# Block-sorted attention and an eight-expert layer on one core: the third batch's queries turned by transposing transfers, its value transfers on ScalarE and GpSimd, and a weight load ahead of four heads of queries

## The chip, the cores and the metric

The kernel runs on one core of one Trainium2 chip. A core has five engines that run their own instruction streams side by side: TensorE (PE, matmuls; its weight loads are listed as PEld), VectorE (DVE), ScalarE (ACT), GpSimd (POOL) and SyncE (SP), which here only starts transfers. Transfers are carried by 16 DMA engines; a transfer is started by an instruction on SP, ACT or POOL and proceeds on its own. The metric is device time in microseconds (us) of one execution; lower is better. Times are medians of several runs, and one further execution is profiled.

## The reference

The first half is attention whose keys and values are mixed block by block with a sort matrix; the second is a layer of eight experts whose routing weights are balanced by rows and columns.

```
B, H, S, D = 4, 8, 768, 64;  8 blocks of 96 rows;  E = 8, F = 1024
P = 5 rounds of (exp(P - max), row normalise, column normalise) of sort_net   # B x H x 8 x 8
k_sorted, v_sorted = einsum('bhij,bhjcd->bhicd', P, k_blocks / v_blocks)
scores = q_block @ k_sorted_block^T / 8      # inside each block of 96
attn   = softmax(scores);  x = attn @ v_sorted_block      # -> 3072 x 512
logits = x @ w_gate;  Pm = exp(logits - max), 8 rounds of row and column normalising
out    = sum_e Pm[:, e] * (relu(x @ w1[e]) @ w2[e])       # 3072 x 512
```

## The kernel before

The four batches of the attention are numbered 0 to 3 (`bb`). For each batch `load_batch` (L72) brings v, k and q from memory, converted to bf16, into tiles `kvq` of 128 partitions by 8 heads by 384 columns (five buffers in turn); row p of a head holds six successive sequence rows, written `(kk d)`. All these loads are started by POOL, one after another, in POOL's program order.

The work on a batch goes in steps, most of them for a pair of heads `hp` (0 to 3):

- `sort_values` (L179, L181): the sort matrix, spread out into `Rt[bb]` by `build_r` (L156), is multiplied with v on PE; ACT copies the products to `vs`. Then `hop` (L172) starts eight transfers that move `vs` to `vsbt[bb % 2]` with a block of 96 rows on 96 partitions. Even ones are started by SP, odd ones by POOL.
- `keys` (k, L218 and L223): sorted keys on PE, copied by DVE into `kTs` with the head dimension on the partitions.
- `queries` (q): the queries are turned so that the head dimension lies on the partitions. For batches 0 and 1 PE turns them head by head (L196). For batches 2 and 3 POOL first copies a pair of heads into a tile `qr` that puts both heads side by side (L201, two buffers), then PE turns six blocks of 128 x 128 (L205). ACT copies the result out of PSUM into `qTs` (L208), with the order of rows restored.
- `scores` (s, L239, L247): a block's keys times its queries on PE; ACT takes the exponential into `atp`.
- `mix` (m, L257, L260, L261): the exponentials times the sorted values on PE; DVE divides by the sum of each row.
- `turn` (t, L268, L271) and `logits` (l, L283): the result is turned into `xtT` and multiplied by `w_gate`.

The string of a `plan` gives the order of these steps (k0 is the keys of pair 0, and so on). Between steps PE works on expert 0 of the second half for the batches already done: `hidden0` (L379, L381), which needs `w1`, and `output0` (L388, L396), which needs `w2`. `weave` and `run_both` set how many of its steps stand between two steps of the attention. All these PSUM tiles come from eight banks in turn.

The order on an engine is the program's order for instructions that go through `pin`; others may be moved by the framework's scheduler. `tc.issue_after(x)` puts the instructions of its block behind instruction x on the same engine. L433 uses that once: POOL copies two numbers of `vsbt[0]` into a small tile `held`, and so waits for the values of batch 0, before it starts the loads of batch 1 and of w1 and w2 of expert 0.

After the attention the remaining seven experts run as a long PE-filled loop (L601, L688) with sums and differences of operands on POOL and DVE; the change does not touch it.

Of the kernel before, what the change touches and what calls it, by code (L numbers as in the profile page):

```python
# [25 lines left out]
def kernel(  # L26
# [40 lines left out]
    def load_batch(bb, parts):  # L67
        for x, l0, n in parts:
            d, src = {"v": (vt, v), "k": (kt, k), "q": (qt, q)}[x]
            if bb not in d:  # L70
                d[bb] = kvp.tile([128, 8, 384], BF16, name="kvq", bufs=5)
            pin(nc.gpsimd.dma_start(  # L72
                out=d[bb][:, l0:l0 + n, :],
                in_=src[bb, l0:l0 + n].rearrange("h (p kk) d -> p h (kk d)", kk=6)))
# [93 lines left out]

    def hop(bb):
        for i in range(NB):  # L170
            eng = nc.gpsimd if i % 2 else nc.sync
            (pin if bb == 0 else lambda ins: ins)(eng.dma_start(  # L172
                out=mkap(vsbt[bb % 2], [[VW, 96], [1, 520]], off=i * 520),
                in_=vs[16 * i:16 * i + 16].rearrange("p kk h d -> p kk (h d)")))

# [12 lines left out]
    def queries(bb, hp, bank, qps=None):  # L188

        if qps is None:  # L190
            qps = bank([128, 6, 128], BF16)
        if bb < 2:

            for kk in range(6):
                for h in range(2):
                    pin(nc.tensor.matmul(qps[64 * h:64 * h + 64, kk, :],  # L196
                                         qt[bb][:, 2 * hp + h, kk * 64:kk * 64 + 64],
                                         Ibig, is_transpose=True, start=True, stop=True))
        else:
            qr = sp.tile([128, 6, 2, 64], BF16, name="qr", bufs=2)  # L200
            nc.gpsimd.tensor_copy(  # L201
                qr.rearrange("p kk h d -> p h kk d"),
                qt[bb][:, 2 * hp:2 * hp + 2].rearrange("p h (kk d) -> p h kk d", d=64))
            for kk in range(6):
                pin(nc.tensor.matmul(qps[:, kk, :], qr[:, kk].rearrange("p h d -> p (h d)"),  # L205
                                     Ibig, is_transpose=True, start=True, stop=True))
        qT[bb, hp] = sp.tile([128, 128, 6], BF16, name="qTs", bufs=4)
        nc.scalar.copy(qT[bb, hp], qps.rearrange("p kk c -> p c kk"))  # L208

    def keys(bb, hp, bank):  # L210

# [14 lines left out]
    at = {}  # L226
# [4 lines left out]
    def scores(bb, hp, bank):  # L231

        for b in range(2):
            sps = [bank([128, 4, 96], F32) for h in range(2)]
            for j in range(4):
                i = 4 * b + j
                for h in range(2):
                    r = slice(64 * h, 64 * h + 64)
                    pin(nc.tensor.matmul(  # L239
                        sps[h][0:96, j, :],  # L240
                        kT[bb, hp][r, i].rearrange("p c kk -> p (c kk)"),
                        qT[bb, hp][r, 16 * i:16 * i + 16].rearrange("p c kk -> p (c kk)"),
                        start=True, stop=True))
            for h in range(2):
                if b == 0:
                    new_at(bb, hp, h)
                nc.scalar.activation(out=at[bb, hp, h][0:96, 4 * b:4 * b + 4],  # L247
                                     in_=sps[h][0:96], func=AF.Exp, scale=scale)

    def mix(bb, hp, h, bank):  # L250
        if h == 0:
# [208 lines left out]
    with ExitStack() as c2:  # L460
# [22 lines left out]
        def run_both(a, counts):  # L483
            for n in counts:
# [9 lines left out]
        run_both(at1, (1, 1, 1, 1, 0, 1, 0, 1, 1, 0, 1))  # L494
        load_batch(2, [(x, 0, 8) for x in "vkq"])
        build_r(2, nc.gpsimd, 4)
        run_both(at1, (1, 1, 1, 1))
        run_both(sort_values(2, bank1), (1, 0, 1, 0, 1))
        run_both(at1, (1, 0, 0, 0))
        usual = "q0,q1,k0 k1,s0,q2 k2,s1,q3 m0 k3,s2 m1,t0 s3 m2,t1 m3 t2 t3,l0 l3"  # L500
        for bb, ns in ((2, (5, 3, 2, 4)), (3, (5, 4, 0, 5))):
            at1 = attention(bb, bank1, usual)
            weave(at1, ex, 5, ns[0])
            if bb + 1 < B:
                load_batch(bb + 1, [(x, 0, 8) for x in "vkq"])
                build_r(bb + 1, nc.gpsimd, 4)
# [12 lines left out]
            weave(at1, ex, 4, ns[3])  # L519
# [311 lines left out]
```

## Time and profile before

| what | value |
|---|---|
| median of 3 runs | 679.78 us (679.38 to 680.32) |
| profiled execution, own time | 679.37 us |
| its span | 677.4 us |
| PE busy | 651.2 us, 96% |
| DVE, ACT, POOL busy | 541.6 (80%), 298.2 (44%), 473.5 (70%) us |
| granted TensorE clock | full in every slice |
| attention, first to last turn into xtT | ends near 112 us |

The span is the stretch from the first to the last recorded instruction; the own time of the execution adds what lies around it. In the order of time a line gives the start and the length in us, the engine, the source line, what is written from what, how many instructions were merged, and in square brackets how long the engine sat idle before them and what ended that. PSUM tiles are named `bank`, `bk` or `oacc`. A transfer's landing is counted from the start of the instruction that starts it.

### The profile page before, as it was taken

How to read it: one execution, taken by the hardware profiler on the slowest of the kernel's cores; microseconds unless marked ns; L12 is line 12 of the kernel's file. 1: busy time of each engine (PE TensorE's matmuls, PEld its weight loads, DVE VectorE, ACT ScalarE, POOL GpSimd, SP SyncE). 2: the span in 40 equal slices, each digit the busy share in tenths (PEclk: the TensorE clock that was granted, in tenths of full speed). 3: DMA queues.
4: the chain of work that ended last, by engine and by line, in shares of the span. 5: the costliest groups of instructions: out<-in, count | busy, mean ns of one | idle time of the engine just before them, and what ended most of it. 6: DMA issues, size and time to landing. Idle time of an engine off the chain costs nothing.

```text
span 677.4 us, 13154 instructions
## 1 busy us (share of the span) xinstructions
PE 651.2 (96%) x5043; PEld 434.7 (64%) x5122; DVE 541.6 (80%) x1131; ACT 298.2 (44%) x541; POOL 473.5 (70%) x499
## 2 busy tenths in 40 slices
PE   4899999999999999999999999999999999999996
PEld 2656766554666666666666666666666666666675
DVE  6617768663788889888888889888898888888896
ACT  4575763469533343434333343333433343333430
POOL 4542435007987988898997898689886999646745
PEclk9999999999999999999999999999999999999999
DMA  9898973101240340030303040034003120001223
GB/s 159 143 215 132 160 133 47 19 1 24 40 62 1 63 63 1 1 63 10 55 1 57 7 64 1 2 63 63 1 1 64 19 45 1 0 1 63 94 78 141
DMA packets 32415, 36.57 MB, mean 54 GB/s; under 512 B 2016, under 2 KB 25312, under 8 KB 32352
## 3 DMA queue, kind: packets, MB, share of 16 engines
q0 software_dynamic: 26912, 27.82, 25.9%
q1 hardware_dynamic: 5440, 7.90, 3.6%
q8 instruction: 40, 0.66, 0.4%
q14 instruction: 23, 0.19, 0.1%
HBM read 52.45 MB, written 6.29 MB: 87 GB/s over the span
## 4 chain that ended last, share of the span: by engine, by line
PE 72%; DVE 1%; issue 1%; POOL 1%; ACT 0%; DVEq 0%
PE oacc L688 37%; PE bk L601 34%; PE bk L688 1%; DVE osbl L653 1%; POOL hs L671 1%; DVE hT L637 0%; DVE hT L640 0%; ACT p L621 0%; DVEq L653 0%
## 5 line engine op out<-in xcount | busy, mean ns | idle before, releaser
L653 DVE SCALAR_TENSOR_TENSOR osbl<-oacc,glog,osbl 128x256 f32<-128x256 f32 (+1 forms) x490 | 255.6, 522 | 61.3 <-PE oacc L688 61.2
L671 POOL TENSOR_TENSOR hs<-hT 128x512 bf16<-128x512 bf16 (+2 forms) x105 | 99.5, 961 | 68.4 <-DVE hT L640 68.2
L601 PE MATMUL bk<-xtT,w1e 128*128 128x512 bf16 x475 | 143.5, 379 | 0.9
L688 PEld LDWEIGHTS <-hT 128*128 128x128 bf16 x1008 | 98.6, 98 | 64.5 <-issue 1.3
L688 PEld LDWEIGHTS <-hs 128*128 128x128 bf16 x1008 | 98.5, 98 | 64.6 <-POOL hs L671 1.5
L688 PE MATMUL oacc<-w2e,hT 128*128 128x256 bf16 x796 | 119.6, 273 | 1.0 <-ACT hT L643 0.5
L643 ACT ACTIVATE hT<-bk 128x512 bf16<-128x512 f32 x84 | 50.3, 599 | 158.7 <-PE bk L601 140.9
L671 POOL TENSOR_TENSOR hs<-hT,hs 128x512 bf16<-128x512 bf16 (+2 forms) x105 | 100.0, 959 | 4.9
L671 POOL TENSOR_TENSOR hs<-hs,hT 128x512 bf16<-128x512 bf16 (+2 forms) x105 | 99.9, 959 | 4.2 <-ACT hT L643 0.4
L601 PE MATMUL bk<-xc,wc 128*128 128x512 bf16 x319 | 96.2, 379 | 0.6 <-ACT p L621 0.2
L688 PE MATMUL oacc<-w2e,hs 128*128 128x256 bf16 x612 | 92.0, 273 | 1.6 <-POOL hs L671 0.9
L629 ACT COPY u<-bk 128x512 f32<-128x512 f32 x84 | 49.3, 587 | 95.2 <-PE bk L601 83.6
L601 PEld LDWEIGHTS <-w1e 128*128 128x128 bf16 x672 | 65.7, 98 | 10.5
L637 DVE CUSTOM_DVE_ANT_0 hT<-bk,p 128x512 bf16<-128x512 f32 x84 | 58.1, 692 | 11.8 <-ACT p L634 6.4
L647 DVE SCALAR_TENSOR_TENSOR h<-bk,hT 128x512 bf16<-128x512 f32 x84 | 57.2, 681 | 5.7 <-ACT hT L643 5.7
L634 ACT COPY p<-bk 128x512 f32<-128x512 f32 x84 | 49.4, 588 | 23.5 <-PE bk L601 23.5
L621 ACT COPY p<-bk 128x512 f32<-128x512 f32 x84 | 49.4, 588 | 20.1 <-PE bk L601 20.1
L625 DVE CUSTOM_DVE_ANT_0 hT<-bk,p 128x512 bf16<-128x512 f32 x84 | 57.2, 681 | 1.1 <-ACT hT L381 0.6
L640 DVE CUSTOM_DVE_ANT_0 hT<-bk,u 128x512 bf16<-128x512 f32 x84 | 57.2, 680 | 1.0 <-PE bk L601 1.0
L688 PE MATMUL oacc<-w2s,hs 128*128 128x256 bf16 x364 | 54.8, 273 | 0.3
L601 PEld LDWEIGHTS <-wc 128*128 128x128 bf16 x504 | 49.3, 98 | 8.0 <-issue 0.4
L601 PE MATMUL bk<-xtT,wc 128*128 128x512 bf16 x159 | 48.0, 379 | 0.0
(136 smaller groups left out, 827.9 us busy)
## 6 DMA issues: line engine op xcount, KB each, us to landing
w2e<-in_moe_w_dram POOLq DMA_DIRECT2D x8, 1024.0 KB, 8.8
w1e<-in_moe_w_dram POOLq DMA_DIRECT2D x7, 1024.0 KB, 8.3
out_dram<-osbl SPq DMA_DIRECT2D x23, 256.0 KB, 2.0
kvq<-in_v_dram POOLq DMA_DIRECT2D x3, 768.0 KB, 9.0
kvq<-in_k_dram POOLq DMA_DIRECT2D x3, 768.0 KB, 11.6
vsb<-vs SPq DMA_DIRECT2D x16, 97.5 KB, 4.5
vsb<-vs POOLq DMA_DIRECT2D x16, 97.5 KB, 4.0
kvq<-in_q_dram POOLq DMA_DIRECT2D x4, 384.0 KB, 9.6
```

The costliest lines, as they stand in the source:

```text
L601: hold(nc.tensor.matmul(ps, wa[:, kk, :], xa[:, kk, :], start=(first and kk == 0), stop=(kk == 1), skip_group_check=True))
L621: nc.scalar.copy(p1, u)
L625: nc.vector._custom_dve(TENSOR_ADD_SAT, out=c11, in0=w, in1=p1, s0=TOP, s1=0.0)
L629: nc.scalar.copy(u2, u)
L634: nc.scalar.copy(p5, v)
L637: nc.vector._custom_dve(TENSOR_ADD_SAT, out=c22, in0=u, in1=p5, s0=TOP, s1=0.0)
L640: nc.vector._custom_dve(TENSOR_ADD_SAT, out=c12, in0=v, in1=u2, s0=TOP, s1=0.0)
L643: nc.scalar.activation(out=c21, in_=u, func=AF.Relu)
L647: nc.vector.scalar_tensor_tensor(out=h3[e, p][:, i, :], in0=u, scalar=0.0, in1=c22, op0=ALU.max, op1=ALU.subtract)
L653: nc.vector.scalar_tensor_tensor(out=o, in0=ps, scalar=glog[:, t, e:e + 1], in1=o, op0=ALU.mult, op1=ALU.add)
L671: nc.gpsimd.tensor_tensor(out=c, in0=a, in1=b, op=o)
L688: nc.tensor.matmul(ps, h[:, fb, :], w[:, fb, :], start=(first and fb == 0), stop=(fb == 3), skip_group_check=True)
```

## The change

Three things change, all in the attention.

1. Batch 2's queries. A new function `queries_across` lets POOL make all four `qr` copies one after another (four buffers instead of two) and lets SP start four transposing transfers from `qr` into `qTs`. `qTs` of batch 2 has its columns in the order (kk c), so the scores take a strided slice of it, their columns come out in that order too, and the exponential reads PSUM at a stride to put them right. The q steps leave the plan of batch 2. POOL's copy of two numbers of the last turned tile into `held` now stands before the loads of batch 3, which are issued behind it. `build_r(2)` stands ahead of batch 2's loads.
2. Batch 2's value transfers: the four that SP started are started by ACT. All transfers of `hop` are now pinned, as are the `qr` copies; on POOL batch 3's four `qr` copies thereby come after batch 3's value transfers instead of two on either side.
3. The loads of batch 1: w2 of expert 0 is loaded ahead of heads 4 to 7 of the queries, and the plan of batch 1 has s1 ahead of q2, and s2 ahead of q3.

In the built order of DVE, one of the differences `xc` (L146) now stands behind four of batch 2's key copies (L223) instead of ahead of them.

```diff
     def hop(bb):
         for i in range(NB):
-            eng = nc.gpsimd if i % 2 else nc.sync
-            (pin if bb == 0 else lambda ins: ins)(eng.dma_start(
+            eng = nc.gpsimd if i % 2 else nc.scalar if bb == 2 else nc.sync
+            pin(eng.dma_start(
...
-            qr = sp.tile([128, 6, 2, 64], BF16, name="qr", bufs=2)
-            nc.gpsimd.tensor_copy(
+            qr = sp.tile([128, 6, 2, 64], BF16, name="qr", bufs=4)
+            pin(nc.gpsimd.tensor_copy(
...
+    def queries_across(bb):
+        for hp in range(4):
+            qr = sp.tile([128, 6, 2, 64], BF16, name="qr", bufs=4)
+            pin(nc.gpsimd.tensor_copy(
+                qr.rearrange("p kk h d -> p h kk d"),
+                qt[bb][:, 2 * hp:2 * hp + 2].rearrange("p h (kk d) -> p h kk d", d=64)))
+            qT[bb, hp] = sp.tile([128, 6, 128], BF16, name="qTs", bufs=4)
+            pin(nc.sync.dma_start_transpose(
+                out=qT[bb, hp], in_=qr.rearrange("p kk h d -> p (kk h d)")))
...
-                        qT[bb, hp][r, 16 * i:16 * i + 16].rearrange("p c kk -> p (c kk)"),
+                        (qT[bb, hp][r, :, 16 * i:16 * i + 16] if bb == 2 else
+                         qT[bb, hp][r, 16 * i:16 * i + 16].rearrange("p c kk -> p (c kk)")),
...
+                to, of = at[bb, hp, h][0:96, 4 * b:4 * b + 4], sps[h][0:96]
+                if bb == 2:
+                    to = to.rearrange("p j (c kk) -> p j c kk", kk=6)
+                    of = of.rearrange("p j (kk c) -> p j c kk", kk=6)
+                nc.scalar.activation(out=to, in_=of, func=AF.Exp, scale=scale)
...
-            load_batch(1, [("v", 0, 8), ("k", 0, 8), ("q", 0, 4), ("q", 4, 4)])
+            load_batch(1, [("v", 0, 8), ("k", 0, 8), ("q", 0, 4)])
             load_w2(0)
+            load_batch(1, [("q", 4, 4)])
...
-        at1 = attention(1, bank1, "k0 k1 k2 q0 q1 s0 q2 s1 k3 q3 s2 "
+        at1 = attention(1, bank1, "k0 k1 k2 q0 q1 s0 s1 q2 k3 s2 q3 "
...
+        build_r(2, nc.gpsimd, 4)
         load_batch(2, [(x, 0, 8) for x in "vkq"])
-        build_r(2, nc.gpsimd, 4)
         run_both(at1, (1, 1, 1, 1))
+        queries_across(2)
         run_both(sort_values(2, bank1), (1, 0, 1, 0, 1))
...
-            at1 = attention(bb, bank1, usual)
+            at1 = attention(bb, bank1, usual if bb == 3 else
+                            "k0 k1,s0 k2,s1 m0 k3,s2 m1,t0 s3 m2,t1 m3 t2 t3,l0 l3")
...
-                load_batch(bb + 1, [(x, 0, 8) for x in "vkq"])
+                turned = pin(nc.gpsimd.tensor_copy(held, qT[2, 3][0:96, 5, 0:2]))
+                with tc.issue_after(turned.ins):
+                    load_batch(bb + 1, [(x, 0, 8) for x in "vkq"])
```

More of the change, by code (lines that the diff above doesn't have):

```diff
@@ L199, in queries @@
         else:
-            qr = sp.tile([128, 6, 2, 64], BF16, name="qr", bufs=2)
-            nc.gpsimd.tensor_copy(
+            qr = sp.tile([128, 6, 2, 64], BF16, name="qr", bufs=4)
+            pin(nc.gpsimd.tensor_copy(
                 qr.rearrange("p kk h d -> p h kk d"),
-                qt[bb][:, 2 * hp:2 * hp + 2].rearrange("p h (kk d) -> p h kk d", d=64))
+                qt[bb][:, 2 * hp:2 * hp + 2].rearrange("p h (kk d) -> p h kk d", d=64)))
             for kk in range(6):
@@ L208, in queries @@
         nc.scalar.copy(qT[bb, hp], qps.rearrange("p kk c -> p c kk"))
+    def queries_across(bb):
[3 more added lines that the diff above has]
+                qr.rearrange("p kk h d -> p h kk d"),
+                qt[bb][:, 2 * hp:2 * hp + 2].rearrange("p h (kk d) -> p h kk d", d=64)))
+            qT[bb, hp] = sp.tile([128, 6, 128], BF16, name="qTs", bufs=4)
+            pin(nc.sync.dma_start_transpose(
+                out=qT[bb, hp], in_=qr.rearrange("p kk h d -> p (kk h d)")))
     def keys(bb, hp, bank):
@@ L246, in scores @@
                     new_at(bb, hp, h)
-                nc.scalar.activation(out=at[bb, hp, h][0:96, 4 * b:4 * b + 4],
-                                     in_=sps[h][0:96], func=AF.Exp, scale=scale)
+                to, of = at[bb, hp, h][0:96, 4 * b:4 * b + 4], sps[h][0:96]
[3 more added lines that the diff above has]
+                nc.scalar.activation(out=to, in_=of, func=AF.Exp, scale=scale)
     def mix(bb, hp, h, bank):
@@ L491 @@
         run_both(sort_values(1, bank1), (1, 1, 1, 1, 0))
-        at1 = attention(1, bank1, "k0 k1 k2 q0 q1 s0 q2 s1 k3 q3 s2 "
+        at1 = attention(1, bank1, "k0 k1 k2 q0 q1 s0 s1 q2 k3 s2 q3 "
                                   "m0 s3 m1,t0 m2,t1 m3 t2 t3,l0 l3")
-        run_both(at1, (1, 1, 1, 1, 0, 1, 0, 1, 1, 0, 1))
+        run_both(at1, (1, 1, 1, 1, 0, 1, 1, 0, 1, 1, 0))
+        build_r(2, nc.gpsimd, 4)
         load_batch(2, [(x, 0, 8) for x in "vkq"])
-        build_r(2, nc.gpsimd, 4)
         run_both(at1, (1, 1, 1, 1))
+        queries_across(2)
         run_both(sort_values(2, bank1), (1, 0, 1, 0, 1))
```

## The prediction

> **What bounds the kernel now.** First the page: the chain that ended last is TensorE (PE) for 72% of the span, and PE is near full in every slice but the first. So a change is worth what it takes out of, or puts into, PE's own order.
>
> ```profile
> PE   4899999999999999999999999999999999999996
> PE 72%; DVE 1%; issue 1%; POOL 1%; ACT 0%; DVEq 0%
> ```
>
> Next PE in order of time from 40 to 95 us, the stretch that the change touches (start, length, engine, line, what, idle before):
>
> ```profile
> 46.88 0.56 PE L239 MATMUL bank<-qTs,kTs 64*96 64x96 bf16 x16
> 48.60 1.02 PE L388 MATMUL bank<-w2e,hTs 128*128 128x512 bf16 x3 [1.17 <-DMA w2e<-in_moe_w_dram]
> ...
> 69.45 0.83 PE L205 MATMUL bank<-Ibig,qr 128*128 128x128 bf16 x12
> 70.21 0.53 PE L218 MATMUL bank<-R,kvq 128*64 128x128 bf16 x12
> ...
> 71.88 0.56 PE L239 MATMUL bank<-qTs,kTs 64*96 64x96 bf16 x16
> 72.37 0.51 PE L205 MATMUL bank<-Ibig,qr 128*128 128x128 bf16 x6
> 72.72 0.81 PE L379 MATMUL bank<-xtT,w1e 128*128 128x384 bf16 x4
> ...
> 74.72 0.49 PE L205 MATMUL bank<-Ibig,qr 128*128 128x128 bf16 x6 [0.24 <-ACT qTs L208]
> 75.05 0.81 PE L379 MATMUL bank<-xtT,w1e 128*128 128x384 bf16 x4
> 75.70 0.87 PE L257 MATMUL bank<-vsb,atp 96*96 96x65 bf16 x16
> ...
> 92.15 0.83 PE L205 MATMUL bank<-Ibig,qr 128*128 128x128 bf16 x12
> ```
>
> PE waits 1.17 us for w2. From start to next start, the L205 turns of batch 2 (the third) take 0.76 + 0.35 + 0.33 us, with 0.24 us of waiting. Batch 3's turns come at 92.15 with no wait. Then GpSimd (POOL) in the same order: its first copy waits for the q load, and the next batch's load is issued behind the last copies.
>
> ```profile
> 62.73 2.22 POOL L201 COPY qr<-kvq 128x768 bf16<-128x768 bf16 x2 [13.07 <-DMA kvq<-in_q_dram]
> 65.89 2.15 POOL L172 DMA_DIRECT2D vsb<-vs  x4 [0.94 <-ACT vs L181]
> ...
> 72.16 0.93 POOL L72 DMA_DIRECT2D kvq<-in_v_dram  x1
> ...
> 88.86 1.59 POOL L201 COPY qr<-kvq 128x768 bf16<-128x768 bf16 x2 [11.90 <-PE bank L268]
> ```
>
> Last the transfers: the SP queue over the span, the landing of batch 3's q (issued 73.96), and that of batch 2's value transfers.
>
> ```profile
> q1 hardware_dynamic: 5440, 7.90, 3.6%
> kvq<-in_q_dram POOLq DMA_DIRECT2D x1, 768.0 KB, 14.4
> vsb<-vs POOLq DMA_DIRECT2D x4, 97.5 KB, 4.0
> DMA to landing us min/median/max: 2.8/4.0/5.5
> ```
>
> From the first issue of batch 3's load to the landing of its q are 73.96 + 14.4 - 72.16 = 16.2 us; PE asks for the product two copies (1.6 us) and a little later. There the slack is small.
>
> **The change, part by part.**
>
> *w2 ahead of four heads of queries.* w2 landed at 48.54 (28.84 + 19.7). The half load of q that now stands behind it is 384 KB; at the 200 GB/s that the transfers reach there it takes 1.9 us, so w2 lands near 46.6, before PE asks at 47.43 (48.60 - 1.17). Saved: 1.17. That half now lands near 48.5; its turn (L196) stands behind s0, half an output, s1 and half an output, at about 49.65. The new order puts s1's four exponentials (0.41 each) ahead of q2's copy on ScalarE (ACT), so s2 waits some 0.35 us; but before, the same stretch up to 56.38 held 0.42 us of small gaps beyond its work (7.78 against 5 x 0.86 + 3 x 0.46 + 2 x 0.49 + 0.70 = 7.36). I take 1.2 saved, bounds 0.8 to 1.4.
>
> *Batch 2's turns off PE.* 0.76 + 0.35 + 0.33 + 0.24 = 1.7 us leave PE before the first mix (75.70). Next to be late is kT for s0: PE would come 0.3 us before DVE's copies of it, which in the new order start when the logits copy ends (70.15), as one 0.69 us xc difference now stands behind four of them: 70.15 + 1.1 = 71.25, against 71.02. So 1.6 saved, bounds 1.3 to 1.7. The four ACT copies (0.80 each) also go.
>
> *What hides the rest.* Sixteen exponentials read PSUM at a stride: ACT's strided L208 copy and its straight L271 copy both took 0.80 for 768 columns, so nothing; ACT, busy 7.6 of 8 us from 72 to 80, loses two copies there. Were the stride to cost 10%, it would be 0.6 us on ACT. Four value transfers move to ACT: 0.57 to 0.70 each on SP, so 2.3 to 2.8 us behind the last values copy, where ACT sat idle 4.45; behind them waits the next hidden copy, which PE makes only near 69.7. On POOL, build_r (2.1 us) goes ahead of batch 2's load: k and q then land by the idle-queue times of batch 3 (11.4 and 14.4 after issue) at 59.3 and 63.2 instead of 58.9 and 62.7; k is first used after 68. Its cover is the backlog of w2 up to 48.5.
>
> *The new chain.* Four copies in a row at 1.1 us (62.73 row) end at 67.1 to 67.6. POOL's half of the value transfers follows: issued 67.1 to 69.3 instead of 65.9 to 68.0, landing (2.8 to 5.5) 72.1 to 74.8, middle 73.3. Mix 0 wants them at 75.70 - 1.2 - 1.6 = 72.9, the last some 0.3 later: a wait of 0 to 1.6, about 0.1. Then POOL's `held` copy waits for the fourth transposing transfer, and behind it stands all of batch 3's load. Call its landing T4. Batch 3's first turn should come at 92.15 - 2.8 = 89.35, the second six at 89.7, so q must land by 88.1 and T4 be at most 88.1 - 16.2 - 0.25 = 71.65. Every later us costs PE one us; waits at mix 0 or at the scores are inside that, not added, since they move the deadline. hop(3) on POOL (2.15) ahead of the copies fits between 84.9, when the values are out of ACT, and q's landing.
>
> *T4* has no row of its own: four transfers of 196 KB. Lower end: the value transfers' rate. 0.79 MB of turns and 0.80 MB of value transfers at the best 250 GB/s of that stretch is 6.3 us from 64.4, so 70.7; the last, issued at 67.1 plus the shortest landing 2.8, gives 69.9: T4 near 70.7. Upper end: by the piece. The SP queue's row gives 0.036 x 677.4 x 16 / 5440 = 72 ns a packet; if each 128-column block of a row is a packet, 768 a transfer over 16 engines are 3.45 us, four 13.8, T4 = 64.0 + 13.8 + about 0.7 = 78.5. SP issuing six blocks a transfer at its 0.57 gives the same 3.4. I take 72.5, nearer the low end, because the nearest row is the value transfer (same queue, SBUF to SBUF, the same bytes in all), with a tail for shorter pieces. It costs 72.5 - 71.65 = 0.85.
>
> **Sum.** Against the profiled execution: 679.37 (span 677.4 and 1.97 around it) - 1.2 - 1.6 + 0.85 = 677.4. The median of the runs, 679.78, lies 0.41 above that execution: 677.8. After 115 us the order is the old one and PE bound, so the gain should arrive at the end whole.
>
> **Rivals.**
> 1. *Turns as fast as value transfers* (T4 up to 71.65): no new wait, 679.8 - 2.8 = 677.0, and 676.6 with both savings at their upper bounds. For it: 250 GB/s in the value transfers. Against: shorter pieces. [...]
> 2. *The wait eats the gain* (T4 73.1 to 75.8): 679.8 - 2.8 + 2.8 = 679.8 at 74.45.
> 3. *The other side: the transfers are slow by the piece.* T4 78.5, load issued 78.75, q in at 95.0, the copies at 96.6; PE's second six would be at 96.6 instead of 92.5: +4.1, 683.9. It decides from T4 = 75.8 on (2.8 + 1.36 behind 71.65). For it: the packet price; against: transfers of many packets overlap in the queue.
> 4. *Blocks one at a time.* If each of the 24 blocks of 128 x 128 were a transfer waited for alone, at the trace's shortest landing on SP (1.7, sort_net), 41 us: T4 105, +31, 710. Nothing in the trace serializes a queue so. [...]
>
> **Chances.** Main case (T4 71.65 to 73.1) 0.30; rival 1 0.17; rival 2 0.16; rival 3 and its neighbours from T4 75.8 to 79 0.29; rival 4 0.04; beyond rival 3, or a wait I have not seen, 0.04. A change of 0.2% (1.36 us) is about what a measurement tells from none: faster 0.47, within 0.16, slower 0.37. Time 677.8, its own range 677.0 to 678.4. Both signs are live, so the range runs from 676.6 to the piece price, 684.0, leaving out rival 4 and what is beyond.
>
> **What would show it.** The w2 wait before L403's first matmul gone; no L205 between 68 and 80; s0 about 70; the first mix near 73. The four landings on SP against 70.4, 71.8, 74.7 and 77.6, when the scores want them. POOL's load issue: at 72 or 73 I am right, at 79 rival 3 is; the price stands on PE as idle time before batch 3's first turns, released by a copy or the q load. Wrong altogether if ACT is held by its four issues past 70, or if the exponentials of batch 2 are longer than 0.41.

## The result, and the profile after

The change made the kernel slower: 682.52 us against 679.85 us for the kernel before, measured on the same chip, 2.7 us by the medians. The recorded ratio, here and below, is not the quotient of the medians; it is 1.0032 with a 95% interval of 1.0021 to 1.0044. Its executions also scatter more, from 679.61 to 684.68 (679.34 to 682.79 before). The profiled execution took 683.75 us (span 681.5), 4.4 us more than the one profiled before (679.37) and 1.2 us more than the median, so the trace shows an execution somewhat longer than most. Since the diff adds lines, the same instructions carry other line numbers in the changed kernel: L379 is L394, L388 is L403, L218 is L229, L239 is L250, L257 is L272.

First the chain of the page, then PE in order of time, in the changed kernel:

```profile
PE 71%; DVE 1%; issue 1%; POOL 1%; ACT 0%; DVEq 0%
```

```profile
48.27 1.02 PE L403 MATMUL bank<-w2e,hTs 128*128 128x512 bf16 x3 [0.64 <-DMA w2e<-in_moe_w_dram]
...
69.55 0.53 PE L229 MATMUL bank<-R,kvq 128*64 128x128 bf16 x12
...
71.21 0.56 PE L250 MATMUL bank<-qTs,kTs 64*96 64x96 bf16 x16
...
74.06 0.33 PE L272 MATMUL bank<-vsb,atp 96*96 96x65 bf16 x4
76.12 0.28 PE L272 MATMUL bank<-vsb,atp 96*96 96x65 bf16 x2 [1.73 <-DMA vsb<-vs]
77.93 0.59 PE L272 MATMUL bank<-vsb,atp 96*96 96x65 bf16 x10 [1.53 <-DMA vsb<-vs]
78.36 0.82 PE L394 MATMUL bank<-xtT,w1e 128*128 128x384 bf16 x4
...
80.69 1.46 PE L394 MATMUL bank<-xtT,w1e 128*128 128x384 bf16 x4
...
87.47 0.48 PE L179 MATMUL bank<-kvq,R 128*128 128x384 bf16 x2 [0.46 <-DMA kvq<-in_v_dram]
...
96.05 0.51 PE L205 MATMUL bank<-Ibig,qr 128*128 128x128 bf16 x6
96.81 0.51 PE L205 MATMUL bank<-Ibig,qr 128*128 128x128 bf16 x6 [0.26 <-POOL qr L201]
```

The chain is still PE's, a point less of it: PE still sets the end, and what was lost must stand on PE as waits or as slower work. Up to the first mix all went as planned: no L205 stands between 68 and 80, and the mix begins at 74.06 against 75.70, 1.64 us earlier. Then PE waits twice inside that one mix, 1.73 + 1.53 = 3.26 us, and for the values, not for a query. What follows is slow too: four hidden matmuls (L394) take 1.46 us at 80.69 where they take 0.82 elsewhere. The windows say why; after the busy us of PE, PEld, DVE, ACT and POOL, the last three figures are the granted clock of PE, the DMA engines' share (over 1 where packets overlap) and GB/s:

```profile
74.00:76.00 2.00, 0.39 (x6) 0.24 (x4) 0.18 (x1) 1.53 (x5) 0.00 (x0) 1.00 0.56 56
76.00:78.00 2.00, 0.35 (x5) 0.28 (x5) 0.00 (x0) 0.00 (x0) 0.00 (x0) 1.00 1.01 148
78.00:80.00 2.00, 2.00 (x28) 1.38 (x29) 1.80 (x8) 0.49 (x1) 1.19 (x3) 0.78 0.00 0
80.00:82.00 2.00, 2.00 (x21) 1.29 (x22) 0.86 (x2) 1.52 (x4) 2.00 (x3) 0.50 0.66 46
82.00:84.00 2.00, 2.00 (x29) 1.55 (x27) 1.42 (x7) 0.59 (x2) 1.77 (x2) 0.87 1.27 196
```

PE is nearly idle from 74 to 78, and from about 79 to 82.5 it gets half its clock, which is 0.22 x 2 + 0.50 x 2 + 0.13 x 2 = 1.7 us of full clock. By the starts of the same matmuls it cost 1.25 us: from the hidden matmuls behind the mix (78.36, before 76.41) to the first turn into xtT (L283 at 82.92, before L268 at 79.72) PE's delay grew from 1.95 to 3.20 us. In the kernel before the clock is full throughout (1.00 in every window from 60 to 86).

The transfers, from the answers on the two lines that start them (the transposing ones at L218, then batch 2's values at L172), and POOL in order of time:

```profile
L218 SPq DMA_TRANSPOSE qTs<-qr x4: 1217/2067/2898, 65.0 to 70.8; - x4
DMA to landing us min/median/max: 2.9/6.7/10.2
```

```profile
L172 ACTq DMA_DIRECT2D vsb<-vs x4: 677/980/1387, 65.6 to 68.5; - x4
L172 POOL DMA_DIRECT2D vsb<-vs x4: 532/540/555, 67.2 to 68.8; - x4
DMA to landing us min/median/max: 3.5/6.5/9.4
```

```profile
63.61 3.66 POOL L214 COPY qr<-kvq 128x768 bf16<-128x768 bf16 x4 [13.78 <-DMA kvq<-in_q_dram]
67.22 2.11 POOL L172 DMA_DIRECT2D vsb<-vs  x4
78.47 0.18 POOL L523 COPY held<-qTs 96x2 bf16<-96x2 bf16 x1 [9.14 <-DMA qTs<-qr]
79.00 0.91 POOL L72 DMA_DIRECT2D kvq<-in_v_dram  x1 [0.35 <-issue]
```

The values took up to 9.4 us from issue to landing (5.5 before), and the third transposing transfer 10.2. In the trace the four transposing transfers are complete at 67.90, 72.31, 78.05 and 78.41, the values on ScalarE at 69.10, 71.19, 76.08 and 77.89, those on GpSimd at 72.45, 73.04, 76.03 and 77.68. The two kinds are in flight together from 66 to 78. Issuing a transposing transfer costs SP 1.33 and 1.22 us for the first two and 2.80 and 2.90 for the last two. Batch 3's load goes out at 79.00 instead of 72.16, and PE waits 0.46 + 0.26 us more for that; by the starts of the same matmuls the two places cost 0.62 + 0.54 = 1.16 us. The page's row of SP's queue went from 5440 packets to:

```profile
q1 hardware_dynamic: 8192, 8.29, 4.2%
```

The four value transfers that left SP are 448 packets (they stand on ScalarE's queue now), so the transposing transfers brought 8192 + 448 - 5440 = 3200, 800 each.

### The profile page after: what moved, and what is told of

It is laid out like the page before. It is cut to its first block, busy times and chain, and to the rows that moved or that the text cites. A ratio compares the mean times of both kernels' runs of the same rounds, so it can differ in the third digit from the quotient of the medians.

```text
span 681.5 us, 13099 instructions
## 1 busy us (share of the span) xinstructions
PE 651.9 (96%) x5019; PEld 434.2 (64%) x5098; DVE 541.9 (80%) x1131; ACT 295.8 (43%) x537; POOL 472.3 (69%) x500
## 3 DMA queue, kind: packets, MB, share of 16 engines
q1 hardware_dynamic: 8192, 8.29, 4.2%
## 4 chain that ended last, share of the span: by engine, by line
PE 71%; DVE 1%; issue 1%; POOL 1%; ACT 0%; DVEq 0%
PE oacc L708 37%; PE bk L621 34%; PE bk L708 1%; DVE osbl L673 1%; POOL hs L691 1%; DVE hT L657 0%; DVE hT L660 0%; ACT p L641 0%; DVEq L673 0%
```

## The theory, and what would tell it from others

My theory after this reading: the loss is the *meeting* of the transposing transfers with the values' transfers, which slow each other down, then PE's idle time, which halves its clock. Rivals: the transposing transfers are slow by themselves; the values are slow because ScalarE issues them or because two hardware queues (SP's and ScalarE's) run at once; the w2 order is worth nothing; the clock falls for some reason other than PE's idle time.

### The w2 order alone

The kernel before, with part 3 of the change:

```diff
-            load_batch(1, [("v", 0, 8), ("k", 0, 8), ("q", 0, 4), ("q", 4, 4)])
+            load_batch(1, [("v", 0, 8), ("k", 0, 8), ("q", 0, 4)])
             load_w2(0)
+            load_batch(1, [("q", 4, 4)])
...
-        at1 = attention(1, bank1, "k0 k1 k2 q0 q1 s0 q2 s1 k3 q3 s2 "
+        at1 = attention(1, bank1, "k0 k1 k2 q0 q1 s0 s1 q2 k3 s2 q3 "
```

> The kernel before with one part of the change alone: w2 loaded ahead of four heads of batch 1's queries, and batch 1's plan with s1 ahead of q2 and s2 ahead of q3. The prediction's step was 1.2 us saved. In the profile of the changed kernel w2's last piece came at 48.23, so that PE still waited 0.64 us for it, 0.28 us for the queries behind it and some for s2, and nothing was left of the saving by s3. Theory 'the order of loads is worth what was predicted, and one late engine took it in that one execution': 0.6 to 1.2 us below the kernel before. Rival 'the saving only moves to the next waits (the query load and s2)': within 0.3 us of before.

Measured: 678.46 us against 679.9 for the kernel before on that chip, ratio 0.9983 (0.9967 to 1.0). PE in order of time, where w2 is first used:

```profile
47.66 1.04 PE L388 MATMUL bank<-w2e,hTs 128*128 128x512 bf16 x4
48.62 0.56 PE L239 MATMUL bank<-qTs,kTs 64*96 64x96 bf16 x16
```

The wait for w2 is gone. The saving is 1.4 us by the medians and 1.3 by the means, a little over what was expected, though the interval just reaches 1. In the profiled execution of the changed kernel it did not show, since there 15 of the 16 parts of w2 had landed by 45.91 and the last only at 48.23. Of the thirteen profiled executions with this order, one for each kernel of this document but the first, three had such a wait (0.64, 0.43 and 1.13 us). So the saving is there in most executions and not in all.

### The value transfers on ScalarE, queries still turned on PE

The last kernel, with ScalarE as the issuer of batch 2's even value transfers:

```diff
-            eng = nc.gpsimd if i % 2 else nc.sync
+            eng = nc.gpsimd if i % 2 else nc.scalar if bb == 2 else nc.sync
```

> The same, and the even value transfers of batch 2 started by ACT instead of SP; the queries of batch 2 stay on PE, so no transposing transfer is in flight. If starting transfers on ACT is itself a burden (it took 4.1 us for four in the changed kernel), ACT is late for batch 2's first query copies (70.0 in the kernel before) and the time is 1 us or more above e1. If those 4.1 us came from meeting the transposing transfers, the four issues take 2.3 to 2.8 us here, the values land in 2.8 to 5.5 us, and the time is within 0.3 us of e1.

Measured: 678.92 us, ratio 0.9976 (0.9964 to 0.9988). The line that starts the values:

```profile
L172 ACTq DMA_DIRECT2D vsb<-vs x4: 606/682/772, 64.2 to 66.4; - x4
DMA to landing us min/median/max: 3.0/4.4/6.0
```

No wait at the first mix, and ScalarE issues in 0.6 to 0.8 us, not in up to 1.39 as beside the transposing transfers. The time is 0.46 us above the run before by the medians and 0.2 below it by the means, so no loss shows. ScalarE as issuer, without transposing transfers, is therefore not the cause; what the changed kernel lost lies in part 1 of the change, with the transposing transfers.

### The two kinds kept apart: values held behind the transposing transfers

The changed kernel; GpSimd and ScalarE each read two numbers of the last turned tile before they issue a value transfer:

```diff
     def hop(bb):
+        if bb == 2:
+            pin(nc.gpsimd.tensor_copy(held, qT[2, 3][0:96, 5, 0:2]))
+            pin(nc.scalar.copy(held_act, qT[2, 3][0:96, 5, 0:2]))
```

> The changed kernel with batch 2's value transfers held on both engines until the fourth transposing transfer has landed, so that the two kinds never meet. Theory 'meeting': the transposing transfers are quick by themselves (the first, alone, landed 2.9 us after its issue) and slow only beside the value transfers. Then the four issues take about 1.3 us each, the fourth lands at 71.5 to 73 instead of 78.4, the values land 3 to 5.5 us after their issue, near 77, and PE still waits some 3 us at mix 0: time 681.5 to 684. Rival 'the turns are slow by themselves from the third on' (their issues took 2.8 and 2.9 us): the fourth lands at 76 or later here too, the values after 81, time 685 or more.

Measured: 683.95 us, ratio 1.0059 (1.0038 to 1.008). The transposing transfers, now alone:

```profile
L221 SPq DMA_TRANSPOSE qTs<-qr x4: 1210/1211/1332, 65.1 to 69.4; - x4
DMA to landing us min/median/max: 2.8/2.8/4.4
```

This is the line that decides between "slow by themselves" and "meeting": alone a transposing transfer is issued in 1.21 us (the first in 1.33) and lands 2.8 us after the start of its issue in the median, 4.4 at most (6.7 and 10.2 beside the values). The fourth landed at 73.79 in place of 78.41, a little past the 71.5 to 73 expected and well short of the rival's 76. The values, issued only from 73.8 on, landed in 4.1 us (median), but the last at 80.53 and not at 73.30 as before the change, and ScalarE's next hidden copy stood behind their issues. PE waits for that copy in one piece, and the kernel is slower still:

```profile
77.02 1.44 PE L398 MATMUL bank<-xtT,w1e 128*128 128x384 bf16 x4 [5.10 <-ACT hTs L400]
```

The clock falls to 0.5 again, from 76.0, before that wait is over, to 82.9.

### All eight value transfers on GpSimd

The changed kernel with another issuer:

```diff
-            eng = nc.gpsimd if i % 2 else nc.scalar if bb == 2 else nc.sync
+            eng = nc.gpsimd if i % 2 or bb == 2 else nc.sync
```

> The changed kernel with all eight value transfers of batch 2 started by POOL, none by ACT, still beside the transposing transfers. Theory 'meeting' (any transfer beside the transposing ones): the fourth transposing transfer lands after 75, a value transfer still takes 7 us or more, PE waits 2 us or more at mix 0, time 681 to 684. Rival 'it is the two hardware queues, SP's and ACT's, that hold each other up': with ACT's queue empty the fourth lands by 73, the values (last issue near 71.5) by 76, PE waits at most 1.5 us, time 679 to 680.5.

Measured: 681.42 us, ratio 1.0019 (1.0007 to 1.0032). PE in the first mix:

```profile
73.48 0.23 PE L272 MATMUL bank<-vsb,atp 96*96 96x65 bf16 x1 [0.17 <-DMA vsb<-vs]
74.09 0.19 PE L272 MATMUL bank<-vsb,atp 96*96 96x65 bf16 x1 [0.38 <-DMA vsb<-vs]
75.06 0.19 PE L272 MATMUL bank<-vsb,atp 96*96 96x65 bf16 x1 [0.79 <-DMA vsb<-vs]
76.11 0.55 PE L272 MATMUL bank<-vsb,atp 96*96 96x65 bf16 x9 [0.86 <-DMA vsb<-vs]
```

With nothing on ScalarE's queue, PE still waits 0.17 + 0.38 + 0.79 + 0.86 = 2.2 us for the values, the last two transposing transfers still cost SP 2.0 and 3.0 us to issue, and the fourth landed at 76.26. So the pair of hardware queues is not needed for the loss; the kinds meet whoever issues them. It is milder here, though: no value transfer took over 6.3 us, where at least 7 was expected (9.4 in the changed kernel), and the time is 1.1 us below the changed kernel's. What that difference is due to stays open.

### The meeting moved to where there is slack: queries loaded first

Batch 2's v had landed by 55.8 and is read at 61.6 in the changed kernel, its k by 59.7 and at 69.6. So the queries can be loaded, copied and turned ahead of both, and the transposing transfers meet these loads instead of the values. The changed kernel, in another order:

```diff
-        load_batch(2, [(x, 0, 8) for x in "vkq"])
-        run_both(at1, (1, 1, 1, 1))
-        queries_across(2)
+        load_batch(2, [(x, 0, 8) for x in "qvk"])
+        queries_across(2)
+        run_both(at1, (1, 1, 1, 1))
```

> The changed kernel with batch 2's queries loaded first (q, v, k in place of v, k, q) and the four copies and transposing transfers moved up right behind these loads, so that they meet the loads of v and k, 8 us of slack before anything of them is needed, and no longer the transfers of the values. In the changed kernel the v of batch 2 had landed by 55.8 and is first read at 61.6, k by 59.7 and first read at 69.6. Theory (the loss of the change is the meeting of the transposing transfers with the values' transfers, and the halved clock behind PE's wait for them): the transposing transfers land between 59 and 66, the values' by 72.5 as where the queries were turned on PE; PE waits under 0.3 us at the first mix, the granted clock stays 1.0 at 76 to 84, the load of batch 3 goes out by 72.5; all of the 1.6 us of PE work removed is then gained on top of the 1.4 us of the w2 order: 678.5 - 1.6 = 676.9 us (676.3 to 677.8). Rival (transposing transfers slow down whatever else flows, the loads too, by the 4 to 6 us that the values lost): v or k lands 4 us late, PE waits for v at 61.6 or k at 69.6 by 1 to 4 us, and the time is 679 to 683.

Measured: 677.14 us against 679.75, ratio 0.9964 (0.9953 to 0.9976). This is faster than both kernels. The two lines that start the transfers, and PE and POOL in order of time:

```profile
L218 SPq DMA_TRANSPOSE qTs<-qr x4: 1328/1884/3299, 57.0 to 64.0; - x4
DMA to landing us min/median/max: 3.8/7.4/8.9
```

```profile
L172 ACTq DMA_DIRECT2D vsb<-vs x4: 606/644/970, 65.9 to 68.3; - x4
DMA to landing us min/median/max: 3.0/4.2/5.1
```

```profile
74.33 0.87 PE L272 MATMUL bank<-vsb,atp 96*96 96x65 bf16 x16
```

```profile
68.39 0.91 POOL L72 DMA_DIRECT2D kvq<-in_v_dram  x1
```

Both sides of the theory can be read here. The transposing transfers are as slow as in the changed kernel (7.4 us median, up to 3.3 us to issue), because they now meet the loads, and the last of the three loads lands 2 us later (65.60 against 63.55). But nobody is waiting for either: the transposing transfers are complete at 65.88, 66.54, 67.20 and 67.81, over three microseconds before the first scores. The values are back at 4.2 us, the first mix runs without a gap, the clock is full (1.00 in every window from 60 to 88), and batch 3's load goes out at 68.39. So the rival was right in that loads and transposing transfers slow each other too, and wrong about the price: a load came 2 us later, not 4 to 6, and nobody waited. (The 74.33 holds 1.13 us of waiting for w2, one of the three executions named above.) This kernel also has the pinned orders and the moved `build_r` of the change, so these are not what cost the changed kernel its time.

### The same order of loads with the queries on PE

The kernel with the w2 order and ScalarE as issuer, whose queries are turned on PE:

```diff
-        load_batch(2, [(x, 0, 8) for x in "vkq"])
+        load_batch(2, [(x, 0, 8) for x in "qvk"])
```

> All queries turned on PE as before the change, with the w2 order, the values' transfers on ScalarE and GpSimd, and batch 2's queries loaded first; against the kernel with the same order of loads whose queries are turned by transposing transfers (677.1 us). Theory (that kernel's gain is the 1.6 us of PE work that the transfers took over; the order of the loads alone gives nothing, since no query, key or value of batch 2 was waited for): within 0.4 us of the kernel with the queries on PE and the loads in the old order, 678.5 to 679.0 us. Rival (the order of the loads itself is the gain): 677.0 to 677.5 us.

Measured: 679.08 us against 679.61, ratio 0.9985 (0.9972 to 0.9998), the same as in the old order (678.92). The order of the loads gives nothing by itself. The difference to the kernel above, 679.08 - 677.14 = 1.9 us (1.4 to the one below, on the same chip), is what the transposing transfers are worth when they are in nobody's way; the prediction's term for it was 1.6.

### Issuer back on SP, queries first

The kernel with the queries loaded first:

```diff
-            eng = nc.gpsimd if i % 2 else nc.scalar if bb == 2 else nc.sync
+            eng = nc.gpsimd if i % 2 else nc.sync
```

> The kernel with the queries loaded first and turned by transfers (677.1 us), its even value transfers of batch 2 back on SP, where they are issued behind the four transposing transfers (the last of these issued by 65.9 in that kernel, when the first values were ready). Theory (with the transposing transfers out of the values' way, ScalarE as issuer is worth nothing): 677.1 us, 676.7 to 677.6, no wait over 0.3 us at the first mix. Rival (SP is held by its transposing transfers past 66 and the values come late): a wait of 0.5 to 2 us at the first mix, 677.7 to 680 us.

Measured: 677.71 us, ratio 0.9964 (0.9953 to 0.9976). By its median that is 0.1 us above the theory's range and 0.57 above the kernel with ScalarE as issuer (0.3 by the means), which the scatter of six executions each (ranges of 1.7 and 1.6 us) doesn't tell from nothing. The trace has none of the rival's wait: the first mix runs without a gap, and SP is through with its last transposing transfer at 64.7, before the first value transfer is issued at 64.8. So no gain from ScalarE as issuer shows here.

### Half the turns, behind the values' issues

The changed kernel with pairs 0 and 1 turned on PE again, and the other two meant to be held by a copy that reads one number of each landed piece:

```diff
+        gate = pin(nc.gpsimd.tensor_copy(
+            landed, mkap(vsbt[0], [[VW, 96], [520, 8]], off=519)))
-        for hp in range(4):
+        for hp in (2, 3):
...
+            with tc.issue_after(gate.ins):
+                pin(nc.sync.dma_start_transpose(
```

> The changed kernel with head pairs 0 and 1 of batch 2 turned on PE as before the change and pairs 2 and 3 by transposing transfers that are held (by a GpSimd copy that reads one element of each of the eight landed pieces) until the values have landed. Theory (meeting): the values land by 72.5 as with all queries on PE, the two transposing transfers are issued at about 71 to 72.5 at 1.2 to 1.3 us each and land by 76, before their scores (about 76 and 80); no wait over 0.3 at the first mix, clock 1.0; PE has 0.8 us less to do than with all four turned on it, and batch 3's load goes out at about 76 in place of 72, which costs 0 to 1.5 us: 678.5 - 0.8 + 0.4 = 678.1 us (677.4 to 679.4). Rival (the transfers are slow by themselves): the second lands past 78, PE waits for it at the third or fourth scores, the load goes out past 78, and the time is 680 to 682.

Measured: 679.11 us, ratio 0.9989 (0.9974 to 1.0004), near the upper end of what the theory gave. But the hold did not hold. `issue_after` orders instructions of the same engine, and the copy is GpSimd's while the transfers are SP's. In the trace SP issues both before the copy has run:

```profile
L225 SPq DMA_TRANSPOSE qTs<-qr x2: 1210/1629/2048, 69.1 to 71.3; - x2
71.69 0.19 POOL L220 COPY landed<-vsb 96x8 bf16<-96x8 bf16 x1 [1.88 <-DMA vsb<-vs]
```

The first went out at 69.08, when six of the eight value transfers were still in flight, and took SP 2.05 us to issue; the second followed at 71.30, and the last value landed at 71.55. They landed 3.3 and 2.7 us after issue, the values in 4.1 (median, 5.0 at most), and there was no wait at the mix. So the kinds were not kept apart here, and a meeting of some 2.5 us with one transposing transfer did the values no harm that shows. PE lost its gain elsewhere (L257 is the scores in this kernel):

```profile
72.11 0.56 PE L257 MATMUL bank<-qTs,kTs 64*96 64x96 bf16 x16 [1.45 <-DVE kTs L241]
```

In the rebuilt order two xc differences of DVE stand ahead of the key copies, and s0 waits 1.45 us for those. That the kinds are fast when kept apart rests on the run with the values held, not on this one, and the time of this one says little.

### Without the hold on batch 3's load

The changed kernel:

```diff
-                turned = pin(nc.gpsimd.tensor_copy(held, qT[2, 3][0:96, 5, 0:2]))
-                with tc.issue_after(turned.ins):
-                    load_batch(bb + 1, [(x, 0, 8) for x in "vkq"])
+                load_batch(bb + 1, [(x, 0, 8) for x in "vkq"])
```

> The changed kernel without the hold on batch 3's load: it goes out at about 70 to 72, behind GpSimd's issues of the values' transfers, while the transposing transfers and the values' are still in flight. Theory (everything in flight beside a transposing transfer slows): the values land 1 to 3 us later still, PE waits 4 to 6 us at the first mix in place of 3.3, what the earlier load saves at batch 3's first reads (0.46 + 0.26 = 0.7 us in the changed kernel) is less than that, and the time is 683 to 685. Rival (only values and transposing transfers meet, a load queues behind them): the wait at the first mix stays 3.3, the 0.7 us is saved, 681.8 us.

Measured: 686.21 us, ratio 1.0103 (1.0082 to 1.0124), beyond what either side gave. With a load issued from 69.98 on, the transposing transfers and the values both get slower still:

```profile
L218 SPq DMA_TRANSPOSE qTs<-qr x4: 1238/2056/3017, 65.7 to 71.5; - x4
DMA to landing us min/median/max: 2.9/9.1/14.1
```

```profile
78.09 0.28 PE L272 MATMUL bank<-vsb,atp 96*96 96x65 bf16 x2 [3.00 <-DMA vsb<-vs]
80.18 0.94 PE L272 MATMUL bank<-vsb,atp 96*96 96x65 bf16 x10 [1.82 <-DMA vsb<-vs]
```

4.8 us of waiting instead of 3.26, and a clock of 0.5 to 0.58 from 78 to 84. In the changed kernel the hold makes PE wait 0.46 + 0.26 us, and without it the kernel is 3.7 us slower by the medians.

### PE kept at work during the wait

The changed kernel, in `mix`:

```diff
+                if (bb, hp, h, b) == (2, 0, 0, 1) and j in (0, 2):
+                    for _ in range(15 if j == 0 else 26):
+                        fill = at[bb, hp, h][0:96].rearrange("p i c -> p (i c)")[:, 0:65 * (4 - j)]
+                        pin(nc.tensor.matmul(ops[0:96, j:4].rearrange("p j x -> p (j x)"),
+                                             Ibig[0:96, 0:96], fill, start=True, stop=True))
```

> The changed kernel with PE kept at work while it waits in the first mix of batch 2: 15 matmuls of 260 columns ahead of the fifth matmul of the mix and 26 of 130 columns ahead of its seventh, about 1.6 and 1.4 us, written to parts of the bank that the mix's own matmuls overwrite. Theory (PE's idle time of 3.3 us is what halves its clock afterwards): the granted clock stays at 1.0 in 76 to 84, the four hidden matmuls behind the mix take 0.82 us and not 1.46, and 1.7 us of the loss come back: 682.5 - 1.7 = 680.8 us (680.2 to 681.5). Rival (the clock falls for another reason, such as the transfers that flow): clock still 0.5 at 79 to 82, 682.5 us or, where the added matmuls outlast the wait, up to 683.5.

Measured: 682.47 us, ratio 1.004 (1.0017 to 1.0063). The clock stayed full in the profiled execution, as the theory says:

```profile
78.00:80.00 2.00, 2.00 (x44) 1.71 (x41) 1.81 (x7) 1.76 (x5) 2.00 (x3) 1.00 0.87 73
80.00:82.00 2.00, 2.00 (x32) 1.26 (x28) 1.68 (x7) 1.36 (x4) 1.41 (x2) 1.00 1.28 197
```

but the median did not fall by the 1.7 us. The added matmuls took 1.84 + 1.65 = 3.49 us here and are in the program whatever the wait is, while the wait differs from one execution to the next (here the values were issued from 64.36 on and the last landed at 75.41, 11.05 us later; in the changed kernel 65.64 and 77.89, 12.25 us). The price of the clock stays open from this run, so in the next two the wait comes from GpSimd's work.

### A wait without any late transfer, bare and filled

The kernel with the queries loaded first; batch 3's load and `build_r` are called ahead of batch 2's steps, and behind them:

```diff
+        def gap():
+            for _ in range(3):
+                pin(nc.gpsimd.tensor_tensor(
+                    out=mkap(Rt[3], [Rt[3].ap[0], [16, 32], [1, 16]], off=512),
+                    in0=mkap(Pb, [Pb.ap[0], [1, 32], [0, 16]], off=28 * 8),
+                    in1=mkap(mask16, [mask16.ap[0], [0, 32], [1, 16]]), op=ALU.mult))
+            one = vsbt[0][0:96, 4 * 520 + 64:4 * 520 + 65]
+            pin(nc.gpsimd.tensor_copy(one, one))
```

> The kernel with the queries loaded first and turned by transfers (677.1 us), with one wait added: GpSimd repeats three times the second half of batch 3's routing tensor (the same values again) behind its real work, and then copies onto itself the one element of the values that the fifth matmul of batch 2's first mix reads, so that PE waits there for about 2.5 to 3.5 us at a time when no transfer is late. Theory (PE's idle time halves its clock behind it): the clock falls to about 0.5 for 3 us behind the wait, and the time is the wait and 1.2 to 1.7 us more: 677.1 + 3.0 + 1.5 = 681.6 us (680.8 to 682.5). Rival (the halved clock in the changed kernel came with the flood of pieces, not with PE's idle time): clock 1.0, 680.1 us (679.5 to 680.7).

and with PE filled through it:

```diff
+                if (bb, hp, h, b, j) == (2, 0, 0, 1, 0):
+                    for _ in range(28):
+                        fill = at[bb, hp, h][0:96].rearrange("p i c -> p (i c)")[:, 0:260]
+                        pin(nc.tensor.matmul(ops[0:96].rearrange("p j x -> p (j x)"),
+                                             Ibig[0:96, 0:96], fill, start=True, stop=True))
```

> The same added wait with PE kept at work through it by 28 matmuls of 260 columns ahead of the matmul that waits, 3.3 us at 0.116 us each, written to the part of the bank that the mix's own matmuls overwrite. Theory: clock 1.0 behind the wait, the time is the wait (or the 3.3 us of added matmuls where these are longer) and nothing more: 677.1 + 3.2 = 680.3 us (679.8 to 680.8), 1.2 to 1.7 us under the kernel with the bare wait. Rival (the clock does not hang on PE's idle time): the same time as with the bare wait, within 0.4 us.

Measured: 682.05 us bare (ratio 1.003, 1.0015 to 1.0044) and 680.57 filled (1.0009, 0.9995 to 1.0024). PE and the windows, bare:

```profile
77.70 1.10 PE L272 MATMUL bank<-vsb,atp 96*96 96x65 bf16 x12 [4.56 <-POOL vsb L530]
```

```profile
78.00:80.00 2.00, 2.00 (x14) 1.03 (x13) 1.09 (x5) 0.00 (x0) 0.00 (x0) 0.50 1.31 203
80.00:82.00 2.00, 2.00 (x31) 1.57 (x31) 1.38 (x3) 1.12 (x3) 0.00 (x0) 0.50 1.32 205
```

and filled:

```profile
77.07 0.69 PE L277 MATMUL bank<-vsb,atp 96*96 96x65 bf16 x12 [0.20 <-POOL vsb L535]
```

```profile
78.00:80.00 2.00, 2.00 (x37) 1.30 (x36) 1.78 (x6) 1.28 (x4) 0.00 (x0) 1.00 1.31 204
80.00:82.00 2.00, 2.00 (x39) 1.55 (x39) 1.80 (x9) 1.36 (x5) 0.00 (x0) 1.00 1.31 206
```

The two have the same work of GpSimd built in; what PE does meanwhile differs. Idle, PE's next work runs at half its clock until about 82; filled, at full clock, and the time is 682.05 - 680.57 = 1.5 us less by the medians (1.3 by the means of twelve executions each). The length of the wait is not quite fixed, since GpSimd starts that work behind the fourth transposing transfer: in the two profiled executions the mix goes on at 77.70 and 77.07, and 0.6 of the 2.6 us between these two executions was there already. From there to the next mix it is 4.76 us bare (to 82.46) and 2.87 filled (to 79.94), so in these traces the halved clock itself costs 1.9 us. So the clock hangs here on PE's idle time, and not on the transfers, of which none was late and which flow as fast in both (203 to 206 GB/s from 78 to 82). Of the single waits, the clock fell with those of 4.56 and 5.10 us, and did not with that of 1.45 (1.00 in every window from 60 to 88). It fell also where shorter waits stand close together: with 1.73 + 1.53 us in the changed kernel, with 3.00 + 1.82 without the hold, and where four of them made 2.2 us between 73 and 76 (the run with all values on GpSimd; 0.50 from 78 to 80). How much idle time it takes is not shown.

## Why the prediction was wrong, point by point

The forecast was 677.8, a gain of 2.0 us, and the measured time is 682.52, a loss of 2.7, inside the range given but on the other side of no change. What failed is the price of the waiting, 0.85 us in the sum, where the trace has 6.0: both kinds of transfer were given landing times from rows in which they do not meet. By its steps:

- **w2 ahead of four heads of queries** (1.2, bounds 0.8 to 1.4): right in most executions, 1.4 us measured alone. It did not foresee that one part of w2 can land over 2 us behind the rest, and then a wait is back.
- **Batch 2's turns off PE** (1.6): right. 1.64 us at the first mix in the trace, 1.4 to 1.9 us by the medians once nothing else was lost.
- **Exponentials at a stride, ScalarE's issuing, build_r** (0): right as far as the runs tell. The four exponentials of a score step take 1.62 us before and after; where they do not meet the transposing transfers, the value transfers on ScalarE show no cost and no gain.
- **The wait at the first mix** ("0 to 1.6, about 0.1", and held to be inside the term of T4): this is the step that failed first. It took the values' landing times from the trace before (2.8 to 5.5 us), where they had the queues nearly to themselves, and only moved their issue. Beside the transposing transfers they took up to 9.4, and the wait measured 3.26 us.
- **T4** (72.5, 0.85 us in the sum): failed, mostly for the same reason. A smaller part is the issue: the last transfer was taken to go out at 67.1, but each holds SP for 1.2 to 1.3 us even alone, so that the fourth went out at 69.39 and landed at 73.79 with no value beside it. By the prediction's own price that is 2.1 us, and most of the gain is gone. Beside the values the fourth went out at 70.83 and landed at 78.41. That this is near the number of rival 3 (78.5) is luck, as its mechanism is not what the runs show: transfers of the same 800 packets each land in 2.8 us alone (4.4 the fourth), where the rival took 3.45 us of packet time for each. The lower end added the bytes of the two kinds and let them flow at 250 GB/s, and so assumed that they share the engines without loss; in the trace 6 to 10 GB/s moved from 73.8 to 75.0, with both kinds unfinished.
- **The price of a late T4** (1 us per us from 71.65 on): nearly right. It gives 6.76 us for 78.41, all waits before included; from the first mix to the first keys of batch 3, PE's delay against the kernel before went from -1.64 to +4.34, 6.0 us. By the starts of the same matmuls these are 3.6 across the first mix, 1.25 for the halved clock behind it and 1.2 at batch 3's first reads. So the number comes near for another reason: the load's lateness, by which the price was reckoned, cost only the last 1.2. With the 6.0 in place of 0.85, and no gain for w2 in that execution, the sum is 679.37 - 1.6 + 6.0 = 683.8; the execution took 683.75, so nothing was lost anywhere else.
- **PE's clock**: not in the prediction. Every wait was priced by its length alone; this one cost 1.25 us on top in the trace, and the bare wait 1.3 to 1.5 more than the filled one.

Rivals 2 and 3 had the loss come through batch 3's load. It stands earlier, at batch 2's own mix, and the late load added only 0.7 us of waiting to it (1.2 by the starts), since PE had by then lost most of the time that the load was late. Rival 1 holds for a single transfer from issue to landing, 2.8 us alone where the values take 2.8 to 5.5, but not for T4, which even alone came at 73.79 and not by 71.65. In the meeting both kinds slow alike, to 6.7 and 6.5 us in the median, from 2.8 and 4.1 where they were kept apart.

What remains open is what in the meeting costs the time. The runs show that it happens whichever engine issues the values, that it happens with loads from memory as with transfers inside SBUF, that all kinds suffer, and that one transposing transfer in the last 2.5 us of the values' flight was not enough for it in the one execution profiled. They do not show where in the DMA engines the pieces wait, nor whether transposing or the many small packets does it: no run put as many plain packets beside the values. The standstill from 73.8 to 75.0 began soon after an instruction load (16 KB, begun at 73.4); whether that had a part was not tried either.

## What to carry to other kernels

A transfer's landing time read from a trace was good here only for the company it had there (the values' median went from 4.0 to 6.5 us): when a new kind of transfer is put in flight beside it, price both by what is in flight with them, or move the new one to a stretch where all that it meets has slack. Here the same transposing transfers made a kernel some 5 us slower beside the values (682.5) than beside loads that nobody was waiting for (677.1; the kernel before took 679.9 and 679.8 on the two chips). And waits of TensorE of 3 to 5 us cost 1.3 to 1.9 us more in clock here, so they are worth more to remove than their length says.

## What the runs showed of the hardware that was not expected

- Transposing transfers of 128 x 768 bf16 alone: 1.21 to 1.33 us of SP's time each to issue, 2.8 us to landing in the median, 4.4 at most. Beside value transfers or loads: up to 3.4 us to issue, up to 10.2 us to landing beside the values, 8.9 beside loads, 14.1 beside both; the others slow as well (values to 5.3 to 7.3 us in the median, from 4.0 to 4.4).
- Issuing is part of it: an issue that takes 1.2 us alone and 2.9 beside others holds SP, so what stands behind it on SP is late before it starts.
- After waits of 1.73 + 1.53 us PE ran at half its clock for about 3.4 us. In the bare wait of 4.56 us the clock fell before the wait was over, at about 75.2, and stayed at 0.5 until 82, twice as long.
- One part of a load can lag: in the changed kernel's profiled execution 15 of w2's 16 parts landed within 1.0 us of each other and the last 2.3 us later. In three of the thirteen profiled executions with w2 loaded early PE waited for it, and in all three the last part came about 2 us or more behind the rest.
